# Folding a convolution's inputs by reading backwards on VectorE instead of mirroring them with matrix products

## The chip, the cores and the metric

The kernel runs on one core of a Trainium2 chip. The core has five instruction streams: TensorE (PE, with PEld for its weight loads), VectorE (DVE), ScalarE (ACT), GpSimd (POOL) and SyncE (SP, which here only issues transfers). The metric is the device time of one execution in microseconds, taken as the median of several runs.

## The reference

For x, k and v of 2048 steps by 1024 channels the reference computes two sequence models and blends them with a gate:

```
g = sigmoid((x * gate_w).sum(-1))
# a: a diagonal complex state model with 1024 states
h[t] = Lam_bar * h[t-1] + B_bar @ x[t]
a[t] = 2 * real(C @ h[t]) + x[t] * Dskip
# b: a short convolution of k, a product, a long convolution
ks   = sum_i k[t - 3 + i] * shift_k[:, 3 - i]        # 4 taps
kv   = ks * v
y    = irfft(rfft(pad(kv)) * rfft(pad(ssm_k)))[:2048] + kv * ssm_D
b    = x * y
out  = g * a + (1 - g) * b
```

The change concerns the way from k, v, ssm_k and ssm_D to the two spectra of the long convolution.

## The kernel before, in words

The channels of the long convolution are worked off in 8 tiles of 128. The 2048 steps of a tile are 4 blocks of 512. Within a block the discrete transform is taken over even and odd parts: the upper 256 steps plus, and minus, the lower 256 steps in reversed order. These sums and differences are called folds. A folded quantity lies in SBUF with the step on the partitions, as two groups of 128 for the even part and two for the odd part, and products with cosine and sine tables (CF, SF) turn it into a spectrum.

The kernel before gets the reversed order from TensorE. `refl` (line 266) is a matrix with ones, or minus ones, on the antidiagonal. A product with it reverses the 128 partitions; which group is read supplies the rest.

- `fold_K` (line 421, tiles 0 to 2): ssm_k of the tile is loaded transposed (`kn`, steps on the partitions). Ten products with `ident`, `refl` and the row of ssm_D build the even and odd parts in PSUM; ScalarE copies them into `eok`. ssm_D is added to the first step, where it acts as a direct path.
- `mirror_K` (line 436, tiles 3 to 7): two products with `refl` and one of a single row give the reversed part; ScalarE copies it (`lo`) and the upper half (`eok`); VectorE subtracts; GpSimd's queue adds `lo` to the other half in a transfer.
- `tap_sums` (line 452): the four taps as 64 products of 128x128 per tile, with k transposed (`kT`, channels on the partitions) as weights and diagonal matrices `dg` as the moving operand. The result has the steps on the partitions.
- `first_times_v` (line 483, tile 0) and `times_v` (line 496): multiply with v, mirror the product (`mirror`, line 476, two products), then form `ev` by a subtraction on VectorE and the sum in `ks`, by VectorE or by a transfer of GpSimd's queue that adds.

`fwd_K` and `fwd_V` (lines 530 and 550) make the spectra (`psk`, `psv`), ScalarE copies them to SBUF (`Kh`, `Vh`, or a borrowed buffer `BT`), `products` (line 563) multiplies them on VectorE into `G`, and `inverse` (line 606) turns `G` back with 64 products per tile (`psz`), copied to `cv` and stored to the DRAM buffer `cv_scr`.

The order is written out by hand. Every engine's instructions go through `put` (line 89), which fixes the order on each engine (so nearly all rows of the profile carry line 91). The helpers are generators that are advanced a step at a time by the loop over tiles at line 848. In iteration c the loop works on the products of tile c, the inverse of c - 1, the K and V spectra of n = c + 1 and the taps and folds of nn = c + 2. SP's queue takes all loads and stores in program order; ACT's queue takes the six small parameter loads at the start (lines 155 to 166). Those parameters lie as rows in one buffer, and small products with `ident` (result `p`, lines 280 to 291) spread them over the partitions. The buffers of `ld` (three), `eo` (one per name) and `ks` limit how early a load or a fold may start.

After the tiles come the products of the state model (`bu`), its scans on VectorE, the products with C (`psy`) and the blend.

Of the kernel before, what the change touches and what calls it, by code (L numbers as in the profile page):

```python
# [20 lines left out]
def kernel(  # L21
# [43 lines left out]
    PAD = 16  # L65

# [6 lines left out]
    cv_scr = dram.tile([D // 128, 128, 4, 4, 128], BF16, name="cv_scr")  # L73
    rot_pool = pool("rot", 1)
# [91 lines left out]
    nc.scalar.dma_start(out=sD, in_=B_ssm_D.rearrange("(o d) -> o d", o=1))  # L166

    lds = {}

    def load(which, c):  # L170
        cc = slice(c * 128, (c + 1) * 128)
        if which == "kn":

            t = ld.tile([128, NT, 128], BF16, name="kn", tag="ld")
            load_t(t, B_ssm_k[cc, :])
        elif which == "v":

            w = 1 if c < 2 else 2
# [4 lines left out]
            move(t.rearrange("p n k d -> p n (k d)"),  # L183
                 vf.rearrange("(n p) d -> p n d", p=128)[:, :, c * 128:(c + w) * 128])
# [14 lines left out]
    for h in range(2):  # L199
        hs, ns = slice(h * S // 2, (h + 1) * S // 2), slice(h * NT // 2, (h + 1) * NT // 2)  # L200
        load_t(kT0[:, PAD + hs.start:PAD + hs.stop], kf[hs, 0:128])
        move(v0[:, ns, 0], vf.rearrange("(n p) d -> p n d", p=128)[:, ns, 0:128])
    lds["kT", 0], lds["v", 0] = kT0, v0[:, :, 0]
    load("kn", 0)
# [61 lines left out]
    refl = consts.tile([128, 2, 128], BF16, name="refl")  # L266
    nc.gpsimd.memset(refl, 0.0)
    for k, v in enumerate((1.0, -1.0)):
        nc.gpsimd.affine_select(out=refl[:, k], in_=refl[:, k], pattern=[[1, 128]], base=-127, channel_multiplier=1,
                                compare_op=ALU.not_equal, fill=v)  # L270
# [20 lines left out]
    mm(psp[:, 0, 0:3 * ND], prow, ident[64:64 + 3 * ND, 64:64 + 3 * ND], True, True)  # L291
# [129 lines left out]
    def fold_K(c):  # L421

        kb = lds.pop(("kn", c)).rearrange("p (a f) d -> p a f d", f=4)
        eo = eos["k", c] = eo_pool.tile([128, 2, 2, 4, 128], BF16, name="eok")
        for mt in range(2):
            ps = ps2([128, 2, 4, 128], "foldk")
            for e in range(2):
                mm(ps[:, e], ident, kb[:, :, 2 + mt], True, False)
                mm(ps[:, e], refl[:, e], kb[:, :, 1 - mt], False, mt == 0)
                if mt == 1:  # L430

                    mm(ps[:, e, 0], refl[0:1, e], sD[:, c * 128:(c + 1) * 128], False, True)
            act(eo[:, :, mt], ps, func=ACT.Copy)
            yield

    def mirror_K(c):

        kb = lds.pop(("kn", c)).rearrange("p (a f) d -> p f a d", f=4)
        ps = ps2([128, 2, 4, 128], "mirror")
        for mt in range(2):  # L440
            mm(ps[:, mt], refl[:, 1], kb[:, 1 - mt], True, mt == 0)
            if mt == 1:
                mm(ps[:, mt, 0], refl[0:1, 1], sD[:, c * 128:(c + 1) * 128], False, True)
        eo = eos["k", c] = eo_pool.tile([128, 2, 2, 4, 128], BF16, name="eok")
        lo = eo_pool.tile([128, 2, 4, 128], BF16, name="lo", bufs=2)
        act(lo, ps, func=ACT.Copy)
        act(eo[:, 1], kb[:, 2:4], func=ACT.Copy)
        yield
        tt(eo[:, 0], kb[:, 2:4], lo, ALU.subtract)
        gather(eo[:, 1], lo)  # L450

    def tap_sums(kT, dg, h):

        ps = ps2([128, 8, 128], "taps")
        for n in range(8):
            t0 = (8 * h + n) * 128
            for i in range(KS):
                k0 = PAD + t0 - i
                mm(ps[:, n], kT[:, k0:k0 + 128], dg[:, i], i == 0, i == KS - 1)
        return ps  # L460
# [7 lines left out]

    def taps(c, dg):
        kT = lds.pop(("kT", c))  # L470
        ks = ks_pool.tile([128, 4, 4, 128], BF16, name="ks")
        for h in range(2):
            act(of_blocks(ks, h), by_block(tap_sums(kT, dg, h)), func=ACT.Copy)
        kss[c] = ks

    def mirror(c):

        ps = ps2([128, 2, 4, 128], "mirror")
        for mt in range(2):
            mm(ps[:, mt], refl[:, 1], kss[c][:, 1 - mt], True, True)  # L480
        return ps

    def first_times_v(c, dg):

        kT, v = lds.pop(("kT", c)), lds.pop(("v", c))
        ks = kss[c] = ks_pool.tile([128, 4, 4, 128], BF16, name="ks")
        for h in range(2):
            tt(of_blocks(ks, h), by_block(tap_sums(kT, dg, h)), by_block(v[:, 8 * h:8 * h + 8]), ALU.mult)
            yield
        lo = mirror(c)  # L490
        e = eo_pool.tile([128, 2, 4, 128], BF16, name="ev")
        tt(e, ks[:, 2:4], lo, ALU.subtract)
        tt(ks[:, 2:4], ks[:, 2:4], lo, ALU.add)
        eos["v", c] = e, ks[:, 2:4]

    def times_v(c):

        ks, v = kss[c], lds.pop(("v", c))
        tt(ks, ks, v.rearrange("p (b q) d -> p q b d", q=4), ALU.mult)
        yield  # L500
        lo = eo_pool.tile([128, 2, 4, 128], BF16, name="lo", bufs=2)
        act(lo, mirror(c), func=ACT.Copy)
        yield
        e = eo_pool.tile([128, 2, 4, 128], BF16, name="ev")
        tt(e, ks[:, 2:4], lo, ALU.subtract)
        if c in (1, NC - 1):
            tt(ks[:, 2:4], ks[:, 2:4], lo, ALU.add)
        else:
            gather(ks[:, 2:4], lo)
        eos["v", c] = e, ks[:, 2:4]  # L510
# [276 lines left out]
    def step(gen):  # L787
        next(gen, None)
# [10 lines left out]
    copy(pcol[:, 0:3], psp[:, 0, 0:3 * ND].rearrange("p (i j) -> p i j", j=ND))  # L799
    copy(gwb, psp[:, 1, KS * ND:(KS + 1) * ND])  # L800
# [8 lines left out]
    act(flat(CF), flat(hf), func=ACT.Sin, bias=pih, scale=-TWO_PI)  # L809
    first = first_times_v(0, dg0)  # L810
# [5 lines left out]
    run(fold_K(0))  # L816
# [26 lines left out]
    run(fold_K(1))  # L843
# [4 lines left out]
    for c in range(NC - 1):  # L848
# [11 lines left out]
        if c == 0:  # L860
# [19 lines left out]
            run(fold_K(nn))  # L880
# [11 lines left out]
        if nn < NC:  # L892
            dg = dgs(nn)
        run(back)
# [7 lines left out]
        fk = none  # L902
# [6 lines left out]
        run(fk)  # L909
# [146 lines left out]
```

## Time and profile before

| | |
|---|---|
| runs | 417.69, 418.14, 424.27 us, median 418.14 us |
| profiled execution | span 413.4 us from the first to the last instruction; its own time around that span is not recorded apart |
| TensorE | busy 404.2 us, granted clock 0.999 |
| VectorE | busy 398.3 us |
| ScalarE | busy 254.9 us |
| transfers | 59.79 MB in 126302 packets |

A page of the profile gives busy shares, the span in 40 slices, and the chain that ended last: from the last instruction back to what released it, step by step. "Idle" in a row is the time for which the engine stood still just ahead of that instruction, and the name behind the arrow is what it waited for. The first part of the span, up to about 154 us, holds the tiles of the long convolution; what follows is the state model. Durations of neighbouring instructions overlap a little, so the pitch in the chain is somewhat shorter than the duration of a row. A DMA share is a mean over 16 engines and can exceed 1 where transfers overlap.

### The profile page before, as it was taken

How to read it: one execution, taken by the hardware profiler on the slowest of the kernel's cores; microseconds unless marked ns; L12 is line 12 of the kernel's file. 1: busy time of each engine (PE TensorE's matmuls, PEld its weight loads, DVE VectorE, ACT ScalarE, POOL GpSimd, SP SyncE). 2: the span in 40 equal slices, each digit the busy share in tenths (PEclk: the TensorE clock that was granted, in tenths of full speed). 3: DMA queues.
4: the chain of work that ended last, by engine and by line, in shares of the span. 5: the costliest groups of instructions: out<-in, count | busy, mean ns of one | idle time of the engine just before them, and what ended most of it. 6: DMA issues, size and time to landing. Idle time of an engine off the chain costs nothing.

```text
span 413.4 us, 6089 instructions
## 1 busy us (share of the span) xinstructions
PE 404.2 (98%) x2377; PEld 202.2 (49%) x2377; DVE 398.3 (96%) x470; ACT 254.9 (62%) x307; POOL 52.4 (13%) x74
## 2 busy tenths in 40 slices
PE   7999999999999999999999999999999999999995
PEld 4556454554646464444445444444444444444442
DVE  7899999999999999999999999999999999999964
ACT  4898979999999999889223235432542344387001
POOL 3010020202020202001000000101100110133100
PEclk9999999999999999999999999999999999999999
DMA  7768099998999994795199981533955564498422
GB/s 154 154 142 204 10 177 227 215 136 168 217 194 235 190 144 101 155 192 133 33 190 188 175 187 27 124 77 81 203 122 133 117 139 127 78 203 175 106 51 102
DMA packets 126302, 59.79 MB, mean 145 GB/s; under 512 B 106041, under 2 KB 112705, under 8 KB 126274
## 3 DMA queue, kind: packets, MB, share of 16 engines
q1 hardware_dynamic: 117664, 42.22, 47.2%
q0 software_dynamic: 8528, 17.17, 25.1%
q8 instruction: 18, 0.29, 0.3%
q14 instruction: 10, 0.08, 0.1%
q10 hardware_dynamic: 82, 0.02, 0.0%
HBM read 12.86 MB, written 8.39 MB: 51 GB/s over the span
## 4 chain that ended last, share of the span: by engine, by line
PE 64%; DVE 27%; issue 4%; ACT 2%; DMA 1%; ACTq 0%; DVEq 0%
PE psy L91 27%; PE bu L91 27%; DVE wkh L91 8%; DVE BT L91 7%; DVE G L91 6%; PE psz L91 5%; DVE t L91 3%; PE psk L91 2%; DVE ks L91 2%; PE taps L91 1%; DVE ev L91 1%; PE psv L91 1%; PE p L91 1%; DMA rows<-in_A_Lambda_im_dram 1%; PE foldk L91 1%
## 5 line engine op out<-in xcount | busy, mean ns | idle before, releaser
L91 PE MATMUL bu<-xT,BT 128*128 128x512 bf16 x512 | 112.5, 379 | 0.0
L91 PE MATMUL psy<-CT,hb 128*128 128x512 bf16 x512 | 112.0, 379 | 0.0
L91 PEld LDWEIGHTS <-BT 128*128 128x128 bf16 x512 | 50.0, 98 | 60.2
L91 PEld LDWEIGHTS <-hb 128*128 128x128 bf16 x512 | 49.9, 98 | 60.0
L91 ACT ACTIVATE U<-bu 128x1024 bf16<-128x1024 f32 x32 | 32.4, 1020 | 48.2 <-PE bu L91 45.8
L91 DVE TENSOR_TENSOR_SCAN W<-rv,init,A 128x512 bf16<-128x512 f32 x48 | 57.7, 1262 | 0.0
L91 PE MATMUL psz<-G,SI 128*128 128x512 bf16 x128 | 48.5, 379 | 1.9 <-DVE G L91 1.9
L91 PE MATMUL psz<-G,CI 128*128 128x512 bf16 x128 | 48.5, 379 | 0.0
L91 ACT ACTIVATE ga<-psy,gcols 128x1024 bf16<-128x1024 f32 x8 | 8.9, 1113 | 46.3 <-PE psy L91 46.3
L91 PE MATMUL taps<-dg,kT 128*128 128x128 bf16 x512 | 31.8, 226 | 0.0
L91 PEld LDWEIGHTS <-kT 128*128 128x128 bf16 x512 | 30.6, 101 | 0.7
L91 ACT ACTIVATE Vh<-psv 128x1024 bf16<-128x1024 f32 x32 | 30.3, 1041 | 0.0
L91 POOL DMA_DIRECT2D pbb<-gd x12 | 10.3, 856 | 131.5 <-ACT gd L91 119.4
L91 PE MATMUL psk<-eok,CF 128*128 128x512 bf16 (+1 forms) x96 | 25.7, 361 | 0.4 <-ACT eok L91 0.4
L91 PE MATMUL psk<-eok,SF 128*128 128x512 bf16 (+1 forms) x96 | 24.2, 361 | 0.0
L91 ACT ACTIVATE BT<-psy,gcols 128x1024 bf16<-128x1024 f32 x5 | 5.6, 1113 | 29.9 <-PE psy L91 29.9
L91 PEld LDWEIGHTS <-SF 128*128 128x128 bf16 x160 | 15.7, 98 | 16.0 <-issue 0.6
L91 PEld LDWEIGHTS <-CF 128*128 128x128 bf16 x160 | 15.3, 98 | 14.4
L91 DVE TENSOR_TENSOR wkh<-BT,Vh 128x3072 bf16<-128x3072 bf16 (+4 forms) x20 | 21.8, 1112 | 0.0
L91 DVE TENSOR_TENSOR wkh<-Kh,Vh 128x3072 bf16<-128x3072 bf16 (+2 forms) x16 | 21.3, 1352 | 0.0
L91 PEld LDWEIGHTS <-CI 128*128 128x128 bf16 x128 | 12.5, 98 | 17.9 <-issue 3.3
L91 DVE TENSOR_TENSOR hb<-TCS,W 128x2048 bf16<-128x2048 bf16 (+1 forms) x17 | 19.8, 1162 | 1.2
(148 smaller groups left out, 654.9 us busy)
## 6 DMA issues: line engine op xcount, KB each, us to landing
G<-wkh POOLq DMA_DIRECT2D x6, 768.0 KB, 7.2
cv_scr<-cv SPq DMA_DIRECT2D x16, 256.0 KB, 6.3
v<-in_B_v_dram SPq DMA_DIRECT2D x3, 1024.0 KB
pbb<-cv_scr SPq DMA_DIRECT2D x12, 256.0 KB, 3.2
xr<-in_A_x_dram SPq DMA_DIRECT2D x12, 256.0 KB, 3.6
pbb<-gd POOLq DMA_DIRECT2D x12, 256.0 KB, 3.9
TCSi<-m POOLq DMA_DIRECT2D x8, 256.0 KB, 7.5
ga<-xr POOLq DMA_DIRECT2D x8, 256.0 KB, 3.3
```

The source lines that it names most:

```text
L91: i = f(*a, **kw)
```

## The change

No reversal is made by TensorE any more; `refl`, `mirror` and `mirror_K` are gone. Three things take their place.

- K is loaded as it lies (channels on the partitions, a plain transfer). VectorE adds ssm_D to the first column, and forms sum and difference of the upper half and the lower half, which it reads backwards. A transposing transfer from SBUF to SBUF, on SP's queue, brings the result into `eok`. All eight tiles use this.
- For the taps, ScalarE copies the lower part of each block of `kT` backwards into `kR`; the products for the lower two groups take their weights from `kR`, so that they come out reversed.
- v's lower halves must then be reversed as well: two transfers on ACT's queue copy them in reversed order of the rows to a DRAM buffer `vR` (first 256 channels, then the other 768), and every load of v becomes four transfers, two from `vR` and two from v.

ssm_D is loaded as eight rows behind the state parameters and spread over the partitions by the same product. The parameter rows move from the constants to a rotating buffer. The load of the first K stands directly behind the first half of k on SP's queue.

```
+    vR = dram.tile([4, 256, D], BF16, name="vR")
...
-    rows_ = consts.tile([96, D], BF16, name="rows")
-    sD = rows_[0:1]
+    rows_ = u4([96, D], BF16, "rows")
...
-    prow = rows_[64:64 + 3 * ND, 0:128]
+    prow = rows_[64:64 + 4 * ND, 0:128]
...
-    nc.scalar.dma_start(out=sD, in_=B_ssm_D.rearrange("(o d) -> o d", o=1))
+    for cc in (slice(0, 256), slice(256, D)):
+        put("act", nc.scalar.dma_start, out=vR[:, :, cc],
+            in_=vf.rearrange("(b t) d -> b t d", b=4)[:, 0:256, cc][:, ::-1])
+    sDr = rows_[64 + 3 * ND:64 + 4 * ND, 0:128]
+    nc.scalar.dma_start(out=sDr, in_=B_ssm_D.rearrange("(j p) -> j p", p=128))
...
+    def load_v(t, c, w, blocks=range(4)):
+        b0, b1 = blocks[0], blocks[-1] + 1
+        rows = vf.rearrange("(b m p) d -> p b m d", p=128, m=4)
+        back = vR.rearrange("b (m p) d -> p b m d", p=128)
+        tb = t.rearrange("p (b m) d -> p b m d", m=4)
+        cc = slice(c * 128, (c + w) * 128)
+        for m in range(2):
+            move(tb[:, b0:b1, m], back[:, b0:b1, m, cc])
+        for m in range(2, 4):
+            move(tb[:, b0:b1, m], rows[:, b0:b1, m, cc])
...
-            t = ld.tile([128, NT, 128], BF16, name="kn", tag="ld")
-            load_t(t, B_ssm_k[cc, :])
+            t = ld.tile([128, S], BF16, name="kn", tag="ld")
+            move(t, B_ssm_k[cc, :])
...
-    mm(psp[:, 0, 0:3 * ND], prow, ident[64:64 + 3 * ND, 64:64 + 3 * ND], True, True)
+    mm(psp[:, 0, 0:4 * ND], prow, ident[64:64 + 4 * ND, 64:64 + 4 * ND], True, True)
...
     def fold_K(c):
+        kn = lds.pop(("kn", c))
+        tt(kn[:, 0:1], kn[:, 0:1], sDc[:, c:c + 1], ALU.add)
+        kb = kn.rearrange("p (a h t) -> p a h t", a=4, h=2)
+        hi, lo = kb[:, :, 1], kb[:, :, 0, ::-1]
+        f = eo_pool.tile([128, 2, 4, 256], BF16, name="fold")
+        tt(f[:, 0], hi, lo, ALU.add)
+        tt(f[:, 1], hi, lo, ALU.subtract)
+        eo = eo_pool.tile([128, 2, 4, 2, 128], BF16, name="eok")
+        load_t(eo.rearrange("p e a m d -> p (e a m) d"), f.rearrange("p e a t -> p (e a t)"))
+        eos["k", c] = eo.rearrange("p e a m d -> p e m a d")
+
+    def mirrored(kT):
+        kR = ks_pool.tile([128, 4, MR], BF16, name="kR", bufs=1)
+        t0 = PAD + 256 - MR
+        win = kT[:, t0:t0 + S].rearrange("p (b x) -> p b x", x=512)[:, :, 0:MR]
+        act(kR, win[:, :, ::-1], func=ACT.Copy)
+        return kR
...
+                    if m < 2:
+                        w = kR[:, b, 128 * m + i:128 * m + i + 128]
+                    else:
+                        k0 = PAD + 512 * b + 128 * m - i
+                        w = kT[:, k0:k0 + 128]
+                    mm(ps[:, n, m], w, dg[:, i], i == 0, i == KS - 1)
...
+    def fold_v(c, on_dve):
+        ks = kss[c]
+        o = eo_pool.tile([128, 2, 4, 128], BF16, name="ov")
+        tt(o, ks[:, 2:4], ks[:, 0:2], ALU.subtract)
+        if on_dve:
+            tt(ks[:, 2:4], ks[:, 2:4], ks[:, 0:2], ALU.add)
+        else:
+            gather(ks[:, 2:4], ks[:, 0:2])
+        eos["v", c] = ks[:, 2:4], o
...
     act(flat(CF), flat(hf), func=ACT.Sin, bias=pih, scale=-TWO_PI)
+    fold_K(0)
     first = first_times_v(0, dg0)
...
         if nn < NC:
             dg = dgs(nn)
+            kRs[nn] = mirrored(lds["kT", nn])
+            fold_K(nn)
         run(back)
...
-            fk = mirror_K(nn)
-            step(fk)
             taps(nn, dg)
```

More of the change, by code (lines that the diff above doesn't have):

```diff
@@ L201 @@
         load_t(kT0[:, PAD + hs.start:PAD + hs.stop], kf[hs, 0:128])
-        move(v0[:, ns, 0], vf.rearrange("(n p) d -> p n d", p=128)[:, ns, 0:128])
+        if h == 0:
+            load("kn", 0)
+        load_v(v0[:, :, 0], 0, 1, range(2 * h, 2 * h + 2))
     lds["kT", 0], lds["v", 0] = kT0, v0[:, :, 0]
-    load("kn", 0)
     BT = [bt_pool.tile([128, 2, ND, 256], BF16, name=f"BT{g}") for g in range(NG)]
@@ L263, in raise_clock @@
             mm(raised[:, 0], zeros[:, 0:128], zeros, True, True)
[L266 to L270, printed above, removed]
     colm = consts.tile([128, 2], F32, name="colm")
@@ L421, in fold_K @@
     def fold_K(c):
[L423 to L459, printed above, removed]
+        kn = lds.pop(("kn", c))
[3 more added lines that the diff above has]
+        f = eo_pool.tile([128, 2, 4, 256], BF16, name="fold")
@@ new lines, in tap_sums @@
+    def tap_sums(kT, kR, dg, h):
+        ps = ps2([128, 2, 4, 128], "taps")
+        for n in range(2):
+            b = 2 * h + n
+            for m in range(4):
+                for i in range(KS):
+                    if m < 2:
[4 more added lines that the diff above has]
+                    mm(ps[:, n, m], w, dg[:, i], i == 0, i == KS - 1)
@@ L500, in times_v @@
         yield
[L501 to L510, printed above, removed]
+        fold_v(c, c in (1, NC - 1))
     def spectrum(which, c):
@@ L799 @@
     copy(pcol[:, 0:3], psp[:, 0, 0:3 * ND].rearrange("p (i j) -> p i j", j=ND))
+    sDc = consts.tile([128, ND], F32, name="sDc")
+    copy(sDc, psp[:, 0, 3 * ND:4 * ND])
     copy(gwb, psp[:, 1, KS * ND:(KS + 1) * ND])
@@ L842 @@
     step(tv)
-    run(fold_K(1))
+    fold_K(1)
     fwd_V(0, (2, 3))
```

27 lines of the change are left out of this document (9 added, 18 removed).

## The prediction

> **What bounds the kernel now.** I read the page's engine shares and slices first, then the chain of waits in order of time, then a table of stretches. From the page:
>
> ```profile
> span 413.4 us, 6089 instructions
> ...
> PE 404.2 (98%) x2377; PEld 202.2 (49%) x2377; DVE 398.3 (96%) x470; ACT 254.9 (62%) x307; POOL 52.4 (13%) x74
> ...
> PE   7999999999999999999999999999999999999995
> ...
> DVE  7899999999999999999999999999999999999964
> ```
>
> Two engines look full, so shares alone do not name the limit. The chain does (start, length, what; us):
>
> ```profile
> 2.66 3.25 DMA rows<-in_A_Lambda_im_dram
> ...
> 6.04 0.17 PE p L91
> 6.21 5.54 PE taps L91 x64
> 11.74 2.16 PE foldk L91 x10
> ...
> 15.00 2.99 PE psk L91 x15
> ...
> 19.84 1.03 ACT Vh L91
> 20.87 0.94 ACT fa L91
> 21.81 0.95 ACT SI L91
> 22.75 1.84 ACT ks L91 x2
> 24.61 1.23 DVE ks L91
> ...
> 96.81 0.60 DVE ev L91
> ...
> 118.38 0.60 DVE ev L91
> ...
> 151.97 2.37 DVE G L91 x2
> 154.33 0.04 issue
> 154.37 3.40 PE psz L91 x15
> 157.77 0.43 PE mirror L91 x2
> ...
> 353.94 55.27 PE psy L91 x256
> ```
>
> There are three stages. Up to 24.61 a start-up, which hangs on the small parameter loads (the product `p`, line 291, runs at 6.04 when the last of them is there) and then goes through PE and ACT by turns. From 24.61 to 154.33 VectorE, link after link. From 154.37 TensorE to the end. Two stretches of the middle stage, with busy us of PE, PEld, DVE, ACT, POOL, then clock, DMA share and GB/s:
>
> ```profile
> 100.00:110.00 10.00, 10.00 (x97) 6.61 (x96) 10.00 (x13) 8.85 (x10) 1.62 (x3) 1.00 1.07 224
> 110.00:120.00 10.00, 9.70 (x47) 4.40 (x46) 10.00 (x8) 10.00 (x18) 1.91 (x2) 1.00 1.18 191
> ```
>
> And the row of PE's products with G in the tile stage (busy us, mean ns, idle before them, and for whom):
>
> ```profile
> L91 PE MATMUL psz<-G,SI 128*128 128x512 bf16 x93 | 35.2, 379 | 1.9 <-DVE G L91 1.9
> ```
>
> VectorE has no gap, and an iteration takes 21.57 us (from `ev` at 96.81 to `ev` at 118.38); PE has a small gap, in which it waits for VectorE's G. So in the middle stage an instruction added to VectorE moves the handover at 154.37, and whatever moves the handover moves the end, because behind it PE has no idle time to give. Work taken from PE ahead of 154.37 is worth nothing while VectorE is the slower of the two.
>
> **The change part by part.** Start with what TensorE loses, since that is the visible part: three `foldk` groups (2.16 us each), and the mirrors, 0.43 us a pair, eight of v and five of K. Only the mirror of v's last tile, at 157.77, stands behind the handover: **-0.4 us**. The rest lies beside VectorE or in the start-up, where other things take its place.
>
> *VectorE's folds.* Rows by shape (count | busy us, mean ns | idle):
>
> ```profile
> L91 DVE TENSOR_TENSOR eok<-kn,lo 128x1024 bf16<-128x1024 bf16 x5 | 3.4, 686 | 0.0
> L91 DVE TENSOR_TENSOR ev<-ks,mirror 128x1024 bf16<-128x1024 bf16 x1 | 1.2, 1222 | 0.5 <-PE mirror L91 0.5
> L91 ACT ACTIVATE eok<-kn 128x1024 bf16<-128x1024 bf16 x5 | 5.3, 1059 | 0.0
> L91 ACT ACTIVATE lo<-mirror 128x1024 bf16<-128x1024 f32 x12 | 12.4, 1034 | 0.0
> ```
>
> Each tile's fold of K is now a one-column add and two 128x1024 operations, one of whose inputs is read backwards. No row shows a backward read. The bounds are 0.60 us (the pitch of a forward 128x1024 operation in the chain at 96.81; its duration is 686 ns) and 1.14 us (the 1222 ns of the same size at the slow rate, less the same 0.09 overlap). I take 0.60, since type, memory and size are those of the 686 ns row. The add is one of the tiny operations, with a wait for it: 0.2 us as an estimate (0.17 for 128x8, in the row of `thn` below). Seven folds (tiles 1 to 7) fall between 24.61 and 154.33: 7 x (2 x 0.60 + 0.2) = 9.8. Away go five `eok` subtractions, 5 x 0.60 = 3.0. The `ov` subtraction replaces `ev` one for one, and the gather into `ks` stays on GpSimd's queue. Net **+6.8 us**; with 1.14 it is 17.4 - 3.0 = +14.4.
>
> The Trainium skill, "VectorE: DVE Perf Modes", section "What auto-detection actually checks", gives 16-bit operands the double rate at a step of plus or minus one, which by its rule means the 0.60. The Trainium skill, "Vector Engine (DVE) Microarchitecture Reference", section "Performance modes — why throughput varies by op and dtype", lists a negative step among what was not measured. No run here shows it yet.
>
> *The start-up, part one: the parameters.* Rows of the timeline, and of the DMA view of the first 12 us (40 slices of 0.3 us) and of the whole:
>
> ```profile
> 4.17 0.23 ACTq L166 DMA_DIRECT2D rows<-in_B_ssm_D_dram  x1
> ```
>
> ```profile
> GB/s 0 0 0 0 0 24 4 181 211 134 280 89 20 7 222 292 287 285 225 282 155 2 189 282 282 286 251 109 288 290 291 291 48 0 0 0 0 0 0 0
> ```
>
> ```profile
> v<-in_B_v_dram SPq DMA_DIRECT2D x2, 256.0 KB, 4.1
> kn<-in_B_ssm_k_dram SPq DMA_TRANSPOSE x8, 9.5
> ```
>
> ssm_D used to go into a row of its own, needed only by `foldk`. It now is the last eight rows of `prow`, and the one product that spreads all parameters over the partitions waits for it. Its load stands on ACT's queue behind both pieces of the copy that reverses a half of v (2.1 MB, DRAM to DRAM). By the built instruction list it also waits for the second load of v, because it shares that load's semaphore, and that load sits on SP's queue behind the first piece of the copy. So behind ssm_D stand: on PE `p` and all taps; on VectorE the copy of `pcol`, the state parameters and fold 0; on ACT the tables. SP's later loads of v, eok 0 and kT 1 stand behind the second piece as well. This is the costliest step, and the diff hides it in a changed row count.
>
> How long does the copy take? No row shows a copy from DRAM to DRAM. Short end: the 290 GB/s that the loads reach in the first 12 us, 7.2 us for all and 1.8 for the first quarter. Then the first piece lands at about 9 (issue 4.6, 0.6 for issuing, 1.8, and some 2 of latency), the v load 4.1 later, the ssm_D load 3.25 after that (the time of the Lambda_im load): `p` at 16.4 and not 6.04, +10.3. Long end: the copy's reading side is addressed as 4 blocks of 256 rows with a negative step, which do not merge into one run of rows; dealt out by its outermost count it would keep 4 of 16 engines busy, a quarter of 290: 28.9 us. With ssm_D behind it on the same queue (taken to be served in order) `p` comes at 4.6 + 28.9 + 2 = 35.5, +29.5. The 290 belongs to transfers of 128 and more outermost rows; the rows nearest in outermost count are the small loads of eight rows, 2 KB in 3.25 us, far from that rate. So I take the long end: **+29.5 us**, and keep +10.3 for the range. SP's own loads share those engines, which lengthens the copy; its 512 and 1536 byte rows against the loads' 256 shorten it; I let these cancel.
>
> The Trainium skill, "DMA: Bandwidth & Descriptors", section "Why a DMA increments its semaphore by 16 and not by 1", states that a transfer runs on the largest number of engines up to 16 that divides the outermost counts of both its sides: with 4 and 1024 that is four. It speaks against the change; by 16 engines the sum below would be 442. No run here shows it yet.
>
> *The start-up, part two: from `p` to the first full VectorE work.* More rows of the timeline:
>
> ```profile
> 6.95 0.17 DVE L91 TENSOR_SCALAR thn<-abv 128x8 f32<-128x8 f32 x1
> ...
> 7.38 1.22 DVE L91 SCALAR_TENSOR_TENSOR h<-rq 128x1024 f32<-128x1024 f32 x1
> ```
>
> ```profile
> 10.46 1.50 ACT L91 ACTIVATE h<-row,colat,colneg 128x512 f32<-128x512 f16 x2
> ```
>
> ```profile
> 19.54 3.74 PE L91 MATMUL taps<-dg,kT 128*128 128x128 bf16 x64
> ```
>
> Before, the stretch from `p` (6.04) to VectorE's `ks` (24.61) took 18.6 us. After, taps 0 can't start with `p`: half of its weights come from `kR`, which ACT writes behind the tables and the first pair of `h`. Counted from `p`: ACT reaches the end of that pair at 11.96 - 6.04 = 5.9; `kR` 1.06 (the 1059 ns copy; backwards on ACT, bounds 1.0 to 2.1): 7.0; taps 5.54: 12.5; psk 2.99: 15.5; psv, four pairs at the 0.43 of the mirror's pair: 17.2; the last Vh copy 1.03: 18.3; fa and SI 1.89: 20.2; the second `kR` 1.06, on which taps 1 now wait: 21.2; taps 3.6 and the last `ks` copy 1.0: 25.8. Difference **+7.2 us**. It holds if eok 0 has landed by 12.5: fold 0 ends at about 3.9 after `p` (`h`, which ends at 8.60, then 1.4), its transposition up to 9.5 us later, the median of `kn`, which has the same shape. At worst psk waits 1 us. What ACT saves (two `eok` copies, `lo`) is in this count.
>
> *What is hidden.* In the middle stage ACT exchanges three copies a tile (two `lo`, one `eok`, 3.1 us) for one; v's four loads instead of one cost SP some 2 us a pair of tiles; eok comes by a transposition that replaces the transposed load of kn. All of this lies beside VectorE.
>
> *Sum.* 413.4 + 29.5 + 7.2 + 6.8 - 0.4 = 456.5 us of span. The median of the runs, 418.14, is 4.7 above the profiled span (what lies around it): 461.2. I write **460**, 10% slower.
>
> **The rivals.**
>
> *The copy runs on all engines.* For it: nothing in the trace shows a transfer on fewer. The sum is then 413.4 + 10.3 + 7.2 + 6.8 - 0.4 + 4.7 = 442. Chance 0.28.
>
> *Backward reads at the slow rate.* +7.6 for seven folds: 468 with the slow copy, 450 with the fast one. Against it: the type and size of the 686 ns row. Chance 0.12.
>
> *The wait moves to k.* SP issues in program order, and k is needed by:
>
> ```profile
> 100.19 11.80 SPq L91 DMA_TRANSPOSE kn<-in_B_ssm_k_dram  x1
> 112.15 1.93 SPq L91 DMA_TRANSPOSE kT<-in_B_k_dram  x1
> ```
>
> ```profile
> 96.26 1.30 ACT L91 ACTIVATE dg<-ident,pcol 128x128 bf16<-128x128 bf16 x4
> ...
> 103.51 3.75 PE L91 MATMUL taps<-dg,kT 128*128 128x128 bf16 x64
> ```
>
> eok's transposition now stands between two stores of `cv` and waits for the last product with the eok before it (its pool has one buffer); the second store, v, kn and kT queue behind it. kT is wanted sooner too, by `kR` right behind `dg` and ahead of ACT's second copy of `cv`, some 6 us before the taps (103.51 against 97.56). With the DMA share at 1.07 to 1.18 a landing 3 us late in each of five iterations would stop ACT, then PE for want of PSUM, then VectorE: up to +15, 475. For it: 11.80 us for issuing one transposition. Against: ACT is relieved by 2 us an iteration. Chance 0.07.
>
> *Faster.* If TensorE, not VectorE, sets the middle stage, the products it loses count: 3 x 2.16 + 13 x 0.43 = 12.1 us, a time of 406. It needs the reversed copy to stay out of the start as well (ssm_D there by 6 us) and a PE that never waits for VectorE. The waits of psz for G speak against it, the queue order against the other. Chance 0.03.
>
> *It all cancels*, or the parameters do not wait because the load of ssm_D overtakes the copy: then +7.2 and +6.8 less what the relief gives, 425 to 432. Chance 0.04.
>
> **How the numbers follow.** The forecast has 0.46, with a range of its own of 450 to 468. The whole range, 437 to 474, takes in the fast copy and the slow reads. About 2% is what a measurement of this kernel can tell from no change, 410 to 426.5 us. Faster has the one rival, 0.03; within 2%, the lower part of the last, 0.03; slower 0.94.
>
> **What would show it.** `p` near 35 us, not 6, released by the load of ssm_D (16 means the fast copy); on the queue of ACT's transfers about a thousand packets each of 512 and 1536 bytes; `taps` of tile 0 released by ACT's `kR`; VectorE idle until about 60 in the chain, then again without gaps, with `fold` at about 690 ns (1.2 us is the slow rate) and about 22.4 us an iteration where it had 21.6; the handover at about 197; from there to the end 259 us as before less 0.4. The prediction is wrong if `p` stays early, if `fold` costs more than 1.3 us, or if PE or ACT, with kT as releaser, stands in the chain of the middle stage.

## The result and the profile after

| | before | after |
|---|---|---|
| executions in this group | 414.58 to 424.27 us, median 417.91 us (4) | 469.00 to 472.14 us, median 470.02 us (4) |
| profiled execution, span | 413.4 us | 470.4 us |
| TensorE busy, granted clock | 404.2 us, 0.999 | 402.3 us, 0.971 |
| VectorE busy | 398.3 us | 406.5 us |
| ScalarE busy | 254.9 us | 241.4 us |

The changed kernel takes 1.129 times as long (95% interval 1.124 to 1.135), 470.0 us where 460 were forecast. Ratios here and below leave out a few disturbed executions, medians do not; the time of an execution is its span and some 1.7 us more, so that variants are compared by profiled spans. The profiled execution of the kernel after is the longest of its four (472.1 us), so that a gain of a few microseconds against it comes out some 2 us smaller by the medians. The page of the kernel after, in the parts that were shown of before:

```profile
span 470.4 us, 6014 instructions
...
PE 402.3 (86%) x2316; PEld 203.0 (43%) x2316; DVE 406.5 (86%) x490; ACT 241.4 (51%) x292; POOL 47.0 (10%) x66
...
PE   2006665986998989979999999999999999999996
...
DVE  4023749698799999999999999999999999999983
...
PEclk9999796997999989999999999999999999999999
```

TensorE is as busy as before. What is new stands in the left quarter of its slices: two empty ones (a slice is 11.8 us), and sixes and a five in five of the seven behind them, up to 118 us. `PEclk`, the granted clock in tenths, has slices of 6 to 8 up to 176 us, where it was 9 throughout before. The chain of waits, in order of time (start, length, what), tells them apart:

```profile
3.35 10.81 DMA vR<-in_B_v_dram
...
14.67 6.32 DMA v<-vR
...
21.01 11.28 DMA rows<-in_B_ssm_D_dram
...
32.34 0.22 PE p L93
...
38.37 0.97 ACT kR L93
...
39.39 5.66 PE taps L93 x64
...
53.58 0.97 ACT kR L93
...
54.60 6.53 PE taps L93 x64
...
68.81 4.25 DMA eok<-fold
...
73.11 5.38 PE psk L93 x16
...
96.80 11.45 DMA kT<-in_B_k_dram
...
211.61 6.85 PE psz L93 x31
```

Up to `p` it is the copy and what stands behind it. Then, up to 170 us, it goes mostly by PE, ACT and single transfers, where the chain of before ran through VectorE from 24.61 us on. VectorE's own timeline has these gaps between its first product of tile 1 (`ks<-ks,v`) and the handover (start, length, what, and in brackets the idle time ahead of it with its releaser):

```profile
62.22 1.23 DVE L93 TENSOR_TENSOR ks<-ks,v 128x2048 bf16<-128x2048 bf16 x1 [6.17 <-ACT ks L93]
65.92 0.69 DVE L93 TENSOR_TENSOR ov<-ks 128x1024 bf16<-128x1024 bf16 x1 [2.47 <-PE psv L93]
...
89.08 0.17 DVE L93 TENSOR_TENSOR e<-rv,cos 128x8 f32<-128x8 f32 x1 [4.11 <-ACT cos L93]
...
118.98 1.23 DVE L93 TENSOR_TENSOR ks<-ks,v 128x2048 bf16<-128x2048 bf16 x1 [2.55 <-ACT ks L93]
121.38 0.69 DVE L93 TENSOR_TENSOR ov<-ks 128x1024 bf16<-128x1024 bf16 x1 [1.17 <-PE psv L93]
122.65 2.29 DVE L93 TENSOR_TENSOR G<-BT,Vh 128x4096 bf16<-128x4096 bf16 x1 [0.58 <-ACT Vh L93]
```

From 62.22 to the end of G at 211.56 are 149.3 us, of which the last five gaps are 10.9; the work between them is 138.5. Before, the same stretch (24.61 to 154.33) was 129.7 us with no gap. So the 57.0 us of span are: `p` 26.3 later; 11.3 from `p` to `ks` (29.9 for 18.6); 8.7 more work on VectorE; 10.9 of gaps; and -0.2 behind the handover (258.8 for 259.1).

The same cut for every kernel that was run, from the same views ("work" is the stretch less VectorE's gaps; the rest of the span behind it is 258.7 to 260.5 us in all but the last row):

| kernel | span | `p` | `ks` of tile 1 | stretch to handover | gaps | work |
|---|---|---|---|---|---|---|
| before | 413.4 | 6.0 | 24.6 | 129.7 | 0 | 129.7 |
| after | 470.4 | 32.3 | 62.2 | 149.3 | 10.9 | 138.5 |
| copy in 16 groups | 459.7 | 22.8 | 52.1 | 147.4 | 8.9 | 138.5 |
| ssm_D first | 461.4 | 6.8 | 54.9 | 147.8 | 9.3 | 138.5 |
| both of these | 456.4 | 6.5 | 47.4 | 148.7 | 10.2 | 138.5 |
| no copy | 447.5 | 9.1 | 39.1 | 149.5 | 11.0 | 138.5 |
| clock kept up | 465.5 | 32.3 | 57.5 | 149.2 | 10.6 | 138.6 |
| kT early | 463.5 | 30.8 | 60.1 | 143.0 | 4.6 | 138.4 |
| fold 1 early | 464.1 | 33.0 | 62.6 | 142.8 | 5.9 | 136.9 |
| kR late | 468.2 | 32.6 | 61.8 | 145.9 | 7.6 | 138.4 |
| all mending together | 443.4 | 6.8 | 45.3 | 139.3 | 2.5 | 136.8 |
| K's part alone | 423.7 | 7.3 | 26.3 | 138.2 | 1.0 | 137.2 |
| v's part alone | 449.3 | 4.9 | 55.0 | 135.5 | 4.7 | 130.8 |
| K folded without VectorE | 436.1 | 6.6 | 24.9 | 142.4 | 14.7 | 127.7 |

### The profile page after: what moved, and what is told of

Same layout as the page of the kernel before. It is cut to its first block, busy times and chain, and to the rows that moved or that the text cites. A ratio compares the mean times of both kernels' runs of the same rounds, so it can differ in the third digit from the quotient of the medians.

```text
span 470.4 us, 6014 instructions
## 1 busy us (share of the span) xinstructions
PE 402.3 (86%) x2316; PEld 203.0 (43%) x2316; DVE 406.5 (86%) x490; ACT 241.4 (51%) x292; POOL 47.0 (10%) x66
## 4 chain that ended last, share of the span: by engine, by line
PE 69%; DMA 12%; DVE 9%; ACT 5%; issue 2%; SPq 1%; ACTq 1%; DVEq 0%
PE psy L93 24%; PE bu L93 23%; PE psz L93 7%; PE psk L93 6%; PE taps L93 6%; DMA kT<-in_B_k_dram 2%; DMA rows<-in_B_ssm_D_dram 2%; DVE BT L93 2%; DMA vR<-in_B_v_dram 2%; DVE wkh L93 2%; PE psv L93 2%; DVE G L93 2%; DMA kn<-in_B_ssm_k_dram 2%; DMA v<-vR 1%; ACT Vh L93 1%
## 5 line engine op out<-in xcount | busy, mean ns | idle before, releaser
L93 PE MATMUL psz<-G,CI 128*128 128x512 bf16 x128 | 49.6, 387 | 4.3 <-DVE G L93 4.3
L93 PE MATMUL psz<-G,SI 128*128 128x512 bf16 x128 | 49.5, 387 | 3.0 <-DVE G L93 3.0
L93 PE MATMUL psk<-eok,CF 128*128 128x512 bf16 (+1 forms) x96 | 27.4, 381 | 13.1 <-DMA eok<-fold 7.2
L93 PE MATMUL taps<-dg,kR 128*128 128x128 bf16 x256 | 23.8, 247 | 13.9 <-ACT kR L93 13.9
L93 PEld LDWEIGHTS <-kR 128*128 128x128 bf16 x256 | 19.6, 113 | 15.7 <-ACT kR L93 14.9
L93 PE MATMUL psk<-eok,SF 128*128 128x512 bf16 (+1 forms) x96 | 25.8, 380 | 0.0
L93 ACT ACTIVATE ks<-taps 128x1024 bf16<-128x1024 f32 x14 | 14.4, 1025 | 17.0 <-PE taps L93 17.0
L93 ACT ACTIVATE cv<-psz 128x1024 bf16<-128x1024 f32 x16 | 16.2, 1018 | 13.4 <-PE psz L93 13.4
```

Of the source, the lines that this page charges most:

```text
L93: i = f(*a, **kw)
```

## Experiments on the start-up

**The copy in 16 groups.** Is the copy slow because it runs on 4 engines?

```
-    vR = dram.tile([4, 256, D], BF16, name="vR")
+    vR = dram.tile([16, 128, D], BF16, name="vR")
...
-            in_=vf.rearrange("(b t) d -> b t d", b=4)[:, 0:256, cc][:, ::-1])
+            in_=vf.rearrange("(g t) d -> g t d", g=16)[:, :, cc][:, ::-1])
...
-            move(tb[:, b0:b1, m], back[:, b0:b1, m, cc])
+            move(tb[:, b0:b1, m], back[:, b0:b1, 1 - m, cc])
```

> The kernel after the change, but the copy takes all rows of v, reversed within each of 16 groups of 128 rows: twice the bytes (4.2 MB), and 16 as the outermost count on the reading side in place of 4. The loads of v take the group that they need, so the same is computed. Theory (the copy was slow because it ran on 4 engines): with 16 the rate rises from 95 GB/s to 290 or more, both pieces are through in 11 to 15 us and not in 25, `p` starts at 20 to 24 us and not at 32.3, and the time is 458 to 463 us. Rival (a copy from DRAM to DRAM goes at 95 GB/s whatever its outermost count): twice the bytes take 45 us or more, `p` starts later than 50 us, and the time is above 485 us.

Measured: 461.2 us (460.3 to 464.2), 1.112 times before (1.106 to 1.117); `p` at 22.8: the theory. The DMA view in 40 slices of 0.3 to 0.4 us, first of the kernel after from 20 to 32 us, then of this kernel from 4 to 20 us (share of the 16 engines in tenths, and GB/s of all transfers together):

```profile
DMA  2222222222279999999999999992222222210000
GB/s 96 94 95 95 96 100 94 90 96 99 94 111 131 148 130 137 137 136 134 134 139 138 136 136 137 131 151 96 90 96 99 94 96 96 80 34 20 26 26 6
```

```profile
DMA  3599999999999999999999999999999999699999
GB/s 82 154 389 369 308 325 317 337 346 347 348 349 384 371 397 372 353 300 296 330 261 323 303 300 296 326 311 353 311 266 282 342 310 307 204 221 344 323 281 250
```

Loads run beside the copy in a part of both windows. The copy's own queue alone, after the change, moved 0.39 MB from 8 to 13 us, mostly in rows of 512 bytes (79 GB/s), and 0.57 MB from 14 to 20 us, in rows of 1536 (95 GB/s); with 16 groups it moved 1.64 MB from 9 to 14 us, mostly in rows of 1536 (328 GB/s). So twice the bytes are through sooner. The share of the engines' time that its packets took was 25.0% (14 to 20 us) and is 106% here (9 to 14 us), which is four engines' worth of sixteen and then all of them. That is the theory of the outermost count. It is also the Trainium skill's rule ("DMA: Bandwidth & Descriptors", section "Why a DMA increments its semaphore by 16 and not by 1") that the prediction drew on: by it 4 engines for a count of 4 and 16 for a count of 16, a ratio of 4; the shares agree, and the rates have a ratio of 3.5.

**ssm_D first.** The load of ssm_D stands ahead of the copy on ACT's queue.

```
+    sDr = rows_[64 + 3 * ND:64 + 4 * ND, 0:128]
+    nc.scalar.dma_start(out=sDr, in_=B_ssm_D.rearrange("(j p) -> j p", p=128))
     pih = consts.tile([128, 1], F32, name="pih")
...
-    sDr = rows_[64 + 3 * ND:64 + 4 * ND, 0:128]
-    nc.scalar.dma_start(out=sDr, in_=B_ssm_D.rearrange("(j p) -> j p", p=128))
```

> The kernel after the change, but the load of ssm_D is issued ahead of the two pieces of the copy, behind the other parameters. Theory (it is the place of ssm_D behind the copy that holds `p`): `p` starts at 6 to 7 us, as before the change. What is behind it is then held by the next late thing, the second half of k and v, which stand on SP's queue behind loads that wait for the copy: taps of tile 0 at 22 to 26 us (39.4 after the change), VectorE's `ks` of tile 1 at 50 to 55 (62.2), and the time is 458 to 464 us. Rival 1 (nothing but the parameters matters in the start-up): the whole 26 us go, 443 to 447 us. Rival 2 (the copy holds everything through v alone): `ks` of tile 1 stays at 60 or later and the time above 467.

Measured: 462.2 us (460.4 to 463.2), ratio 1.112 (1.108 to 1.117), the theory and neither rival. `p` is 25.5 us earlier, the end of the span only 9.0. The second wait was there all along, on SP's queue; its timeline in this kernel:

```profile
15.81 3.32 SPq L93 DMA_TRANSPOSE kT<-in_B_k_dram  x1
19.18 1.74 SPq L93 DMA_DIRECT2D v<-vR  x2
31.81 0.89 SPq L93 DMA_DIRECT2D v<-in_B_v_dram  x2
32.80 1.89 SPq L93 DMA_TRANSPOSE eok<-fold  x1
```

The loads of v's second half are not all issued until the copy is through, and eok 0 queues behind them.

**Both together.** 

> Both edits of the start-up together: the copy of all rows of v in 16 groups, and the load of ssm_D ahead of it. Theory (each edit left the other's wait standing: with the fast copy alone `p` still waits for it, with ssm_D first alone the second half of v and the eok behind it on SP's queue still wait for it): `p` at 6 to 7 us, the loads of v through by 21 and eok 0 in SBUF by 28, `ks` of tile 1 at 43 to 47 us (62.2 after the change), 447 to 454 us. Rival (the two savings of 9 us are the same 9 us): 458 us or more.

Measured: 454.9 us (453.1 to 458.2), ratio 1.098 (1.087 to 1.108), span 456.4, `p` at 6.5 and `ks` at 47.4, a fraction above what was expected. By medians the two edits alone save 8.8 and 7.9 us and together 15.1; they are nearly independent. What is late now is the second half of kT, which stands behind the first loads of v on SP's queue: ScalarE waits 10.25 us for it ahead of the first kR, at 23.5.

**No copy.** The price of the copy as a whole; the kernel then leaves out the reversal of v:

```
-    for cc in (slice(0, 256), slice(256, D)):
-        put("act", nc.scalar.dma_start, out=vR[:, :, cc],
-            in_=vf.rearrange("(b t) d -> b t d", b=4)[:, 0:256, cc][:, ::-1])
...
-            move(tb[:, b0:b1, m], back[:, b0:b1, m, cc])
+            move(tb[:, b0:b1, m], rows[:, b0:b1, m, cc])
```

> The kernel after the change without the copy that reverses v in DRAM: all four loads of each v take v itself. The reversal of v's lower halves is left out, the instructions of the engines are the same. Theory (the copy is paid in the start-up only; kR, taps behind kR and the waits of the middle stage stay): `p` at 6 to 8 us, `ks` of tile 1 25 to 30 us behind it, the stretch from there to the handover 146 to 150 us as after the change, 436 to 445 us. Rival (the waits of the middle stage also come from the late start and the loads from the copy): that stretch falls to 138 to 142 us, 425 to 435 us.

Measured: 446.8 us (445.9 to 449.3), ratio 1.071 (1.061 to 1.081), a little above the theory's range and far above the rival's. The copy is worth 22.9 us of span, all of it in `p` (23.3 earlier). Work and gaps of the stretch do not change (138.5 and 11.0): they do not come from the copy or the late start. Its chain:

```profile
9.06 0.20 PE p L92
...
16.10 5.75 PE taps L92 x64
...
31.39 6.57 PE taps L92 x64
```

Even without a copy `p` waits till 9.1, 3 us longer than before, and both groups of taps stay slow.

**The clock kept up.** Why are the taps slow? They run right behind a wait of TensorE for kR.

```
     mm(psp[:, 0, 0:4 * ND], prow, ident[64:64 + 4 * ND, 64:64 + 4 * ND], True, True)
+    raise_clock(14)
...
+        keep = [ps2([128, 2, 512], "raised")] if warm else None
+        for _ in range(warm):
+            mm(keep[0][:, 0], CF[:, 0, 0:128], CF[:, 0], True, True)
...
-    taps(1, dg1)
+    taps(1, dg1, 18)
```

> The kernel after the change, with 14 products whose result nobody reads behind `p` and 18 ahead of the taps of tile 1, so that TensorE does not stand idle ahead of them. Theory (the taps of tiles 0 and 1 take 5.7 and 6.5 us in place of 3.7 because the granted clock fell while TensorE waited for kR): taps 0 and taps 1 take 3.7 to 4.2 us each, `ks` of tile 1 comes 3 to 4.7 us earlier, at 57.5 to 59 us, and the time is 465 to 467 us. Rival (the taps are slow because the reversed weights are, or the next wait, for eok 1, takes the gain back): taps stay at 5 us or more, or the time stays at 469 to 471 us.

Measured: 466.9 us (463.7 to 467.3), ratio 1.123 (1.112 to 1.134), span 465.5. The first taps of tile 1 in TensorE's timeline, after and here, and the stretch around them in the table of stretches (busy us of PE, PEld, DVE, ACT, POOL, then clock, DMA share, GB/s), after and here:

```profile
54.60 1.03 PE L93 MATMUL taps<-dg,kR 128*128 128x128 bf16 x8 [4.01 <-ACT kR L93]
```

```profile
52.64 0.62 PE L93 MATMUL taps<-dg,kR 128*128 128x128 bf16 x8
```

```profile
54.00:58.00 4.00, 3.40 (x33) 3.41 (x34) 2.05 (x3) 0.54 (x1) 1.34 (x1) 0.50 0.24 42
```

```profile
52.00:56.00 4.00, 3.87 (x63) 3.38 (x62) 2.10 (x3) 1.61 (x2) 1.34 (x1) 1.00 0.23 40
```

With the same weights and the same data the two groups take 3.76 and 3.75 us for 5.66 and 6.53, and `ks` comes 25.2 us behind `p` in place of 29.9. It is the clock, not the reversed weights: in the slow groups the products with `kT`'s own weights, which are not reversed, are as slow as the others (1.06 us for eight). For the taps of tile 0 only the durations show it; the clock on record reads 1.00 there, in the kernel after (12 products a microsecond from 40 to 42 us, where the full rate is 22) as in the one before. The gaps behind it stay (10.6), so the whole gain of 4.7 reaches the handover.

## Experiments on the stretch of the middle

**Each part alone.** K's part: the kernel before with `fold_K` and the plain load of K as after, ssm_D as eight rows, `rows_` in the rotating buffers and one `lo`. The core of it:

```
-            run(fold_K(nn))
+            fold_K(nn)
...
             dg = dgs(nn)
+            fold_K(nn)
...
-            fk = mirror_K(nn)
-            step(fk)
```

> The kernel before the change, with the K part of it alone: K loaded plainly, ssm_D as eight parameter rows (no copy stands ahead of its load), folded by VectorE reading backwards and transposed from SBUF; v, the taps and the mirrors of v as before the change (with one buffer for `lo` and not two). Theory (VectorE's folds cost their own 6.8 us, and the transposition on SP's queue makes the K spectra of tiles 1 and 2 late, some 5 us more; the copy of v, kR and the cold TensorE are the rest): `p` at 6 to 7 us, 425 to 431 us. Rival 1 (the waits of the middle stage came from kR and the late start alone): 422 to 425. Rival 2 (all 19.6 us of the middle stage come from the way of K): 435 to 440.

Measured: 424.8 us (423.8 to 425.6), ratio 1.023 (1.019 to 1.026). That is the upper edge of rival 1, just below the theory: VectorE's own work is there (7.5 us more), the late K spectra are not (1.0 us of gaps). v's part with K's way of before:

```
     nc.scalar.dma_start(out=sD, in_=B_ssm_D.rearrange("(o d) -> o d", o=1))
+    for cc in (slice(0, 256), slice(256, D)):
+        put("act", nc.scalar.dma_start, out=vR[:, :, cc],
+            in_=vf.rearrange("(b t) d -> b t d", b=4)[:, 0:256, cc][:, ::-1])
...
             dg = dgs(nn)
+            kRs[nn] = mirrored(lds["kT", nn])
```

> The other part alone: the copy that reverses v, kR and the taps from it, v's folds without mirrors, while K keeps the way of the kernel before the change (products with ident and refl, `mirror_K`, ssm_D as a row of its own), with the load of ssm_D ahead of the copy. To be held against the kernel after the change with ssm_D first (462.2 us). Theory (the way of K costs its 9 us on VectorE here too, and the waits come from v and kR): 450 to 457 us. Rival (the waits of the middle stage come from eok on SP's queue and go with it): 438 to 446 us.

Measured: 452.6 us (451.1 to 453.0), ratio 1.084 (1.074 to 1.093), in the theory's range. The work on VectorE grows by 7.5 us with K's part and 1.1 with v's, together 8.6 of the 8.7 of the whole change. The gaps do not add: 1.0 and 4.7 alone, 10.9 together. The 4.7 is VectorE's wait for `psv` ahead of `ov` of tile 1 (2.5 in the kernel after): `ov` has one buffer, and TensorE's products with the `ov` before it run behind the taps of tile 1. Neither part alone has the gap of 4.1 us at 89 us or those at 119 to 123. That fits a wait for kT that needs both parts, a ScalarE that wants kT early (for kR) and a queue in which kT stands behind eok; the next experiment tries it.

**kT early.** kT of the next tile is loaded ahead of the transposition.

```
             kRs[nn] = mirrored(lds["kT", nn])
+            if nn + 1 < NC:
+                load("kT", nn + 1)
             fold_K(nn)
```

> The kernel after the change, but kT of tiles 3 to 7 is loaded one iteration earlier on SP's queue, ahead of the transposition of the fold before it. Theory (in iteration c = 1 `kR` on ScalarE waits 9.4 us for kT, which queues behind eok and kn; that costs VectorE the idle time at 119 to 123 us): the wait falls to 0, and 3 to 7 us go: 463 to 467 us. Rival (VectorE and TensorE find the next wait, for the K spectra or for kn, which is now loaded behind kT): 468 to 474 us.

In the profiled execution ScalarE's wait of 9.39 us is gone, and with it the last three gaps of VectorE (4.3 us). The gap for `cos` is 2.0 us shorter, as the taps of tile 2 ran at the full clock here (3.76 us, 5.11 after the change); that is not the edit's doing, for with the copy in 16 groups or ssm_D first they took 3.76 too, and without the copy 5.12. ScalarE's timelines, after and here:

```profile
108.32 1.07 ACT L93 ACTIVATE kR<-kT 128x1040 bf16<-128x1040 bf16 x1 [9.39 <-DMA kT<-in_B_k_dram]
```

```profile
94.68 1.10 ACT L93 ACTIVATE kR<-kT 128x1040 bf16<-128x1040 bf16 x1
```

The span is 6.9 us shorter (2.1 of it ahead of `ks`, 6.4 in the stretch, 1.6 lost behind it), but the four executions took 465.3, 465.4, 470.1 and 470.7 us, median 467.7, ratio 1.128 (1.114 to 1.143). That the wait and the gaps go is shown; that the gain is there in every execution is not.

**Fold 1 early.** Fold 1 stands ahead of VectorE's product `ks<-ks,v` of tile 1.

```
     tv = times_v(1)
+    fold_K(1)
     step(tv)
     fwd_K(0, (2, 3))
     step(tv)
-    fold_K(1)
```

> The kernel after the change, with VectorE's fold of K of tile 1 ahead of its product with v, while it waits for the taps of tile 1 anyway. Theory (TensorE stands for 7.2 us ahead of the K spectra of tile 1 because fold 1 comes late and its transposition takes 4.3 us; the products behind it then run at half the clock, and VectorE waits 4.1 us for ScalarE's `cos` behind them): the wait falls to 2 to 4 us, 2 to 5 us faster, 465 to 468 us. Rival (VectorE's next wait, for kT of iteration c = 1, takes it back): 469 to 472 us.

Measured: 466.7 us (464.1 to 467.6), ratio 1.117 (1.107 to 1.128), span 464.1: the theory. TensorE's wait for eok 1 falls from 7.23 to 2.65 us, the gap for `cos` disappears, and the fold itself (1.6 us) goes into time in which VectorE waited anyway: work 136.9.

**kR late.** kR directly ahead of the taps.

```
-            kRs[nn] = mirrored(lds["kT", nn])
```

> The kernel after the change, but in the iterations from c = 1 on `kR` is written directly ahead of the taps (behind ScalarE's copies of the K spectrum) and not ahead of the second copy of `cv`. Theory (ScalarE's wait for kT in front of that `kR`, 9.4 us in iteration c = 1, is a part of the 12.8 us that the middle stage lost beyond VectorE's own work): 3 to 8 us faster, 462 to 467 us. Rival (the later `kR` only moves the wait to the taps, about 1.3 us in each of five iterations, and VectorE sets the pace anyway): 468 to 477 us.

Measured: 472.3 us (469.3 to 474.8), ratio 1.139 (1.129 to 1.149), no gain: the rival. The chain now stays on TensorE from the taps at 107 us to the end; one iteration:

```profile
175.57 1.07 ACT kR L93
...
176.68 5.38 PE taps L93 x64
182.06 3.45 PE psv L93 x16
185.51 6.91 PE psz L93 x32
192.42 6.07 PE psk L93 x32
...
199.43 1.07 ACT kR L93
```

Two microseconds without work, between `psk` and the taps, were followed by taps of 5.38 us in place of 3.75: this iteration takes 23.9 us, more than VectorE's 22.7. It is not so each time: behind the same wait the taps at 130.59 took 3.75.

**All mending together.** The copy in 16 groups, ssm_D first, kT early, 32 products for the clock, fold 1 early. 

> The kernel after the change with all the mending at once: the copy in 16 groups, ssm_D ahead of it, kT one iteration earlier, the products that keep TensorE's clock up ahead of the first taps, and fold 1 ahead of VectorE's first product of tile 1. Theory (these waits follow one another on one chain, so that the savings add): from the span of 456.4 us with the first two, 6.4 for kT, 3 to 4 for the clock and 3 to 4.5 for fold 1: 441 to 446 us, and VectorE without a gap from iteration c = 1 on. Rival (each removed wait uncovers another): 449 us or more.

Span 443.4 us, as the theory had it, with one gap left (2.5) and work 136.8. But the four executions took 445.2, 446.8, 452.9 and 454.4 us, median 449.9, and the ratio of 1.078 (1.058 to 1.098) is wide: the sum is borne out by two executions, the profiled one among them, not by all. The gap that is left is the wait for `psv` ahead of `ov` of tile 1. The profiled execution is 30.0 us longer than before, 20.7 of them ahead of `ks`, since the loads of v and of the second half of k still wait for the copy.

**K folded without VectorE.** If VectorE is the bound of the stretch, does taking K's fold from it beat the kernel before? Tiles 3 to 7 only:

```
+        act(f[:, 0], lo, func=ACT.Copy)
+        gather(f[:, 0], hi)
+        act(f[:, 1], lo, func=ACT.Identity, scale=-1.0)
+        gather(f[:, 1], hi)
```

> The kernel before the change, with the way of K changed for tiles 3 to 7 only and without VectorE: K loaded plainly, ScalarE adds ssm_D and writes the reversed lower half with both signs, two transfers of GpSimd's queue add the upper half, and a transposition from SBUF brings the result to eok behind the next products. Theory (VectorE sets the middle stage, and each instruction taken from it there moves the handover): five subtractions of 0.60 us go from VectorE, 2 to 4 us faster than before the change: a ratio of 0.990 to 0.996. Rival 1 (TensorE is as full and takes over as the bound): a ratio of 0.997 to 1.003. Rival 2 (the longer chain of ScalarE, two transfers and a transposition makes eok late, and SP's queue stands behind it): a ratio above 1.005.

Measured: 439.1 us (435.2 to 441.8), ratio 1.058 (1.045 to 1.070): rival 2. VectorE's work falls by 2.0 us, and 14.7 of gaps come. Its chain:

```profile
84.83 15.29 DMA fold<-kn
...
100.25 7.29 DMA eok<-fold
...
107.58 7.56 PE psk L91 x32
```

The adding transfers land in 5.3 us by the median of the page; the 15.3 here is the longest of the ten. SP's queue was issuing the transposing loads of the state model's `BT` from 74.83 to 89.42 us; whether these held it is not shown. No variant beats the kernel before.

## Why the prediction was right and where it was wrong

The side, the rough size and the main place were right: slower by about a tenth, most of it in the start-up, through a load that stands behind a copy. The 460 are 10 us short of 470.0, which lies outside the 450 to 468 of the forecast's own mechanism and only inside the whole range. That the 468 of the slow backward reads is the nearest number is chance; their reason is out (below). One of the prediction's own signs of being wrong came: ScalarE's `kR`, released by kT, stands in the chain of the middle stage (96.80 to 108.32). By its steps:

- **The parameters, +29.5.** Measured +26.3: `p` at 32.3 for 35.5. The long end was the right one, and for its reason, four engines' worth: the copy's 2.1 MB went from about 4 to about 30.6 us, 79 GB/s on the mean, where a quarter of 290 is 73. As an attribution it was too simple: ssm_D is one of two waits of nearly the same length. Taking it out of the queue gives back 9.0 and not 26, since v, kT and eok on SP's queue wait for the same copy; the prediction named them and gave them no time of their own. Without the copy 22.9 go, and 3 of the 26.3 stay.
- **From `p` to `ks`, +7.2.** Measured +11.3; the term was mis-sized by 4.1. Of these, 2.9 are the taps of tile 1 (6.53 us for 3.6): the 3.6 comes from a row in which TensorE had been busy, and here it stands at half the clock. Most of the rest had piled up before them: `psv` starts 3.6 us behind the taps of tile 0, released by VectorE's sum into `ks`, where the prediction has the 3.0 of `psk`. The taps of tile 0 were right (5.66 for 5.54), because the row they came from was as slow (12 products a microsecond in its first part). With the clock kept up in both groups the stretch takes 25.2 us.
- **VectorE's folds, +6.8.** Measured +8.7 (7.5 by K, 1.1 by v). Backward reads are as fast as forward ones, as taken. The pitch of an iteration is 22.69 us and not 22.4: the subtraction `eok` had stood between the two last additions into G, and `ev` behind another instruction. Without them an instruction follows the one whose result it reads. From VectorE's timeline of after, the pairs in question:

```profile
166.10 1.22 DVE L93 TENSOR_TENSOR ks<-ks,v 128x2048 bf16<-128x2048 bf16 x1
167.42 0.69 DVE L93 TENSOR_TENSOR ov<-ks 128x1024 bf16<-128x1024 bf16 x1
...
185.25 1.22 DVE L93 TENSOR_TENSOR G<-G,wkh 128x2048 bf16<-128x2048 bf16 x1
186.51 2.36 DVE L93 TENSOR_TENSOR G<-G,BT 128x2048 bf16<-128x2048 bf16 x2
```

  `ks` to `ov` takes 1.32 us and `G` to `G` 1.26. From VectorE's timeline of before, the same two ahead of an instruction that does not need their result:

```profile
107.08 1.22 DVE L91 TENSOR_TENSOR G<-G,wkh 128x2048 bf16<-128x2048 bf16 x1
108.22 0.69 DVE L91 TENSOR_TENSOR eok<-kn,lo 128x1024 bf16<-128x1024 bf16 x1
...
111.09 1.22 DVE L91 TENSOR_TENSOR ks<-ks,v 128x2048 bf16<-128x2048 bf16 x1
112.23 2.29 DVE L91 TENSOR_TENSOR G<-BT,Vh 128x4096 bf16<-128x4096 bf16 x1
```

  That is 1.14 both times, so 0.18 and 0.12 more an iteration, 5 x 0.30 = 1.5 of the 1.9 us. Each part alone has its own half of it (`ks` to `ov` 1.33 with v's part, `G` to `G` 1.25 with K's). That the reading of the result is the cause is inferred from these pairs; the order alone was not changed in any run.
- **"All of this lies beside VectorE."** This step failed: 10.9 us of gaps where none were forecast. Three waits make them: 2.5 for the one buffer of `ov`, 4.1 behind eok 1 (a fold that came late on VectorE, 4.25 us of transposition, then products at half the clock), and 4.3 for kT in iteration c = 1. Fold 1 early takes the second away and kT early the third; the first stayed in all kernels with v's part. The third is the rival "the wait moves to k", named with its queue and its engines and given 0.07: it came once and not in five iterations, 4.3 us and not 15.
- **Behind the handover, -0.4.** Measured -0.2.
- **Span to time, +4.7.** That was the distance of one execution from a median of others. The executions show 1.7 to 1.8 between a span and its own time, so that the profiled one of before took some 415.2 us.

Three terms were 2 to 11 us too low, the gaps most of all, and one 3 too high, so that 456.5 of span stand against 470.4. The rival with the copy on all engines (442) is out by the slow copy itself; the experiment with 16 groups comes to 461 and not to 442, with `p` at 22.8 for the 16.4 of that rival (twice the bytes) and the clock and the gaps on top. Backward reads at the slow rate are out by these rows of after (VectorE's fold, ScalarE's kR):

```profile
L93 DVE TENSOR_TENSOR fold<-kn 128x1024 bf16<-128x1024 bf16 x16 | 10.3, 688 | 0.3
```

```profile
L93 ACT ACTIVATE kR<-kT 128x1040 bf16<-128x1040 bf16 x8 | 8.5, 1062 | 10.5 <-DMA kT<-in_B_k_dram 10.5
```

## What to carry to other kernels

When a transfer is put ahead of a small load, list everything that waits for either on every queue, and price the second wait as carefully as the first: taking one away gave 9 of 26 us here. A stage that is bound by one engine stays so only as long as the others are never late; look for a new wait of an engine in front of a group of products, because it costs its length and may cost the products behind it half their clock. And where a removed instruction stood between two that depend on each other, count less than its own time as saved (here 0.12 of 0.60 us came back as a longer pitch).

## What the runs showed of the hardware

- A copy from DRAM to DRAM whose reading side has an outermost count of 4 moves 79 GB/s (rows of mostly 512 bytes) to 95 GB/s (rows of 1536), with packets that take a quarter of the 16 engines' time; with a count of 16 it moves 328 GB/s (rows of mostly 1536) on all of them.
- An operand read backwards costs VectorE nothing at 16 bits (688 ns for 686) and ScalarE next to nothing (1062 ns for 1059).
- TensorE's granted clock was 0.50 behind a wait of 4.0 us, and the first eight taps behind it took 1.03 us, not 0.62. The Trainium skill, "TensorE: Matmul & The Clock Gate", section "What's actually happening", puts the fall behind an idle window of some 3.4 us that runs on its own, so that the phase decides. That the phase decides agrees: behind the same 3.0 us ahead of the taps of tile 2 these took 5.11 us after the change and 3.76 with kT early, and in the kernel with kR late the same 2.07 us made 3.75 once and 5.37 or 5.38 in three other iterations. The length does not agree: 2.07 us is shorter than that window, and the clock still fell, to 0.52 from 178 to 179 us, when the taps had been running again since 176.68. What counts as idle stays open.
- A transposition of 512 KB from SBUF to SBUF lands in 4.3 us where little else runs (eok 1), and a load of 2 KB behind a large copy on its queue in 11.3, some 9.6 of them while the copy was still running.
